# The first two pairs of a fused linear attention and MLP kernel, cut into single tiles of 128 tokens

## The chip, the cores and the metric

The kernel runs on one core of one Trainium2 chip. The metric is the device time of one execution in microseconds. The time before is 217.22 us, the median of three runs (215.41, 217.22 and 218.05).

## The reference

Linear attention with a decay per head is followed by a normalised MLP with a residual. `q`, `k`, `v` are float32 of shape (4, 8, 768, 64): batch, heads, tokens, head width.

```python
for b in range(nb):                      # blocks of 64 tokens
    intra = einsum('bhic,bhjc->bhij', qb, kb) * Dmask      # lam ** (i - j), causal
    intra = einsum('bhij,bhjd->bhid', intra, vb)
    inter = einsum('bhid,bhde->bhie', qb * lam_pow, kv_state)
    out[:, :, sl] = intra + inter
    kv_state = lam_block * kv_state + einsum('bhsd,bhse->bhde', kb * rev_pow, vb)
x = attn_out as (4, 768, 512)
xn = (x - mean) / sqrt(var + 1e-6) * g_ln
out = x + max(xn @ w_ch1, 0) @ w_ch2     # 512 -> 2048 -> 512
```

## The kernel before, in words

The 3072 tokens are worked as 12 pairs `u` of 256 tokens (pair `u` is chunk `u // 4` of batch `u % 4`). A pair holds two chunks `ab` of 128 tokens; partition `64 * ab + p` holds two neighbouring tokens `j` of all eight heads. Heads are counted as four pairs `p` of heads, `e` being the odd or even one. The work of one pair goes in steps:

- `load_window` issues k, q and v on SP's queue (pair 0 in two parts of four heads, the others whole), in runs of 512 bytes.
- `in_k`, `in_q`, `in_v` cast to bf16 and scale by powers of the decay (`lam_q`, `lam_v`). q carries the growing power and v the falling one, so a mask of zeros and ones (`keep`) is all that the scores need.
- `transpose_pe` turns k and q over on TensorE, or for later pairs `transpose_dma` through SP's queue.
- `scores`, `mask`, `av` are the part inside a chunk; `kv`, `new_state`, `state_sum`, `inter` are the state of 64 by 64 per head and its use. The sums stand in two PSUM tiles, `po0` for chunk 0 and `po1` for chunk 1. Between the two halves of `inter` a small read (`reader`, L417) makes TensorE wait, unless other work stands there.
- `norm` takes mean and variance (L430, L431) and writes the centred, weighted `xc` (L435); `to_xT` transposes it, on TensorE with a copy by ScalarE (L455, L456) for the first two pairs, by DMA (L451) for the others. `rstd_of` takes the root on ScalarE (L461) and the reciprocal on VectorE (L463); it is wanted only by `finish` (L543), since a positive factor passes through the maximum.
- The MLP of pair `g`: `m1` makes two of the 16 feature blocks for 256 tokens (8 matmuls of 256 columns, L484), `m1.tile(c, i)` four blocks, those of quarter `c` of W1, for the 128 tokens `i` alone (16 matmuls of 128 columns, L496). ScalarE's maximum with zero brings the result to `hT` (L487, L499). `m2` (L522) sums four products per part against one quarter of W2.

W1 and W2 are each loaded in four quarters by `load_w1` and `load_w2` on GpSimd's queue, with a cast to bf16. `behind` puts a small copy on GpSimd in front of such a load, so that the load is issued only when the named tile has landed.

The scheduler is told to keep the order of the code, so each engine gets its instructions in the order in which the code issues them. The first two pairs, with the first MLP products between their steps, are written out by hand; from then on a list `plan` of MLP steps runs, and `after` hangs the attention steps of later pairs behind its places (`add(12, ...)`). Buffers set further waits: four PSUM tiles `mm` serve transposes, states and MLP products alike.

## Time and profile before

| | us |
|---|---|
| median of three runs (lowest, highest) | 217.22 (215.41, 218.05) |
| span of the profiled execution, first to last instruction | 214.9 |
| TensorE busy in the span | 201.9 (94%) |
| VectorE, ScalarE, GpSimd busy | 102.9, 87.1, 79.4 |
| first transposes on TensorE | 6.09 |
| first MLP product (L496) | 15.82 |
| first step of the plan (L484) | 31.09 |
| first product with W2 (L522) | 37.68 |
| last matmul ends | 211.06 |

The span and the times of lines are from one profiled execution; the runs' times are of whole executions without the profiler, so the two differ by what lies around the span and by the spread of the runs: 2.3 us from the span to the median. TensorE is busy nearly all the time from 6 us on, so the times above tell at what point of its work it stands.

### The profile page before, as it was taken

What the parts mean: (1) busy time and instruction counts of PE and PEld (TensorE: products, weight loads), DVE (VectorE), ACT (ScalarE), POOL (GpSimd) and SP (SyncE); (2) the same over time, 40 slices, a digit from 0 to 9 for tenths busy, and PEclk for the clock granted to TensorE, in tenths of its full rate; (3) what the DMA queues carried; (4) which work ended last, traced back from release to release, by engine and by line L of the source; (5) the groups of instructions that cost most, each with busy time, mean ns of one, the idle gap of its engine ahead of it and who ended that gap; (6) DMA issues with size and microseconds to landing.
All of it is one profiled execution on the core that took longest, in us unless ns stands there. A gap on an engine that the chain in (4) does not pass through costs nothing.

```text
span 214.9 us, 6642 instructions
## 1 busy us (share of the span) xinstructions
PE 201.9 (94%) x2884; PEld 138.2 (64%) x2899; DVE 102.9 (48%) x225; ACT 87.1 (41%) x165; POOL 79.4 (37%) x111
## 2 busy tenths in 40 slices
...
GB/s 130 289 272 207 219 263 160 236 284 234 215 303 208 169 229 153 110 215 209 126 220 199 137 230 200 177 203 198 206 246 131 128 27 27 99 52 0 98 3 95
DMA packets 94142, 37.13 MB, mean 173 GB/s; under 512 B 68385, under 2 KB 91169, under 8 KB 94114
## 3 DMA queue, kind: packets, MB, share of 16 engines
...
q0 software_dynamic: 4224, 4.19, 12.4%
q8 instruction: 22, 0.36, 0.7%
q10 hardware_dynamic: 306, 0.14, 0.3%
...
## 4 chain that ended last, share of the span: by engine, by line
PE 75%; DMA 13%; POOL 4%; SPq 3%; DVE 2%; issue 1%; POOLq 0%
PE pm L484 35%; PE pm L522 30%; DMA vin<-in_v_dram 6%; DMA qin<-in_q_dram 4%; SPq L71 3%; DMA kqT<-kq 2%; POOL kq L210 2%; POOL vb L216 2%; PE pm2h L513 2%; PE po L406 1%; PE po L393 1%; PE sc L247 1%; PE po L380 1%; PE sc L327 1%; PE pm1t L496 1%
## 5 line engine op out<-in xcount | busy, mean ns | idle before, releaser
L487 ACT ACTIVATE hT<-pm 128x512 bf16<-128x512 f32 x92 | 54.9, 601 | 91.2 <-PE pm L484 91.0
L484 PE MATMUL pm<-xT,w 128*128 128x256 bf16 x736 | 86.3, 273 | 1.9 <-DMA xT<-xc 1.2
L522 PE MATMUL pm<-w,hT 128*128 128x512 bf16 x353 | 81.1, 379 | 1.0 <-issue 0.3
L484 PEld LDWEIGHTS <-w 128*128 128x128 bf16 x736 | 69.8, 98 | 13.8 <-DMA xT<-xc 1.7
L522 PEld LDWEIGHTS <-hT 128*128 128x128 bf16 x368 | 35.5, 98 | 40.0
L543 DVE SCALAR_TENSOR_TENSOR o<-pm,rstd,x 128x512 f32<-128x512 f32 x23 | 17.1, 748 | 43.5 <-PE pm L522 43.4
L287 POOL TENSOR_TENSOR Sn<-Stmp,lam_s 128x256 bf16<-128x256 f32 x16 | 9.7, 611 | 69.7 <-DVE Stmp L365 49.0
L435 DVE SCALAR_TENSOR_TENSOR xc<-po,mv,g_row 128x512 bf16<-128x512 f32 (+1 forms) x24 | 16.8, 706 | 1.8
L257 DVE TENSOR_TENSOR mA<-sc,keep 128x512 bf16<-128x512 f32 x20 | 13.1, 685 | 6.8 <-PE sc L247 6.7
L428 ACT COPY x<-po 128x512 f32<-128x512 f32 x18 | 9.9, 588 | 11.3 <-PE po L393 5.3
L430 DVE BATCH_NORM_STATS2 stats<-x 128x6 f32<-128x512 f32 x18 | 12.4, 688 | 3.9 <-ACT x L428 3.9
L417 DVE COPY seen<-po 128x8 f32<-128x8 f32 x18 | 2.3, 162 | 23.2 <-PE po L406 23.2
L216 POOL TENSOR_TENSOR vb<-vin,lam_v 128x1024 bf16<-128x1024 f32 (+1 forms) x7 | 11.8, 1696 | 3.7 <-DMA vin<-in_v_dram 3.7
L210 POOL TENSOR_TENSOR kq<-qin,lam_q 128x512 bf16<-128x512 f32 x10 | 10.3, 1045 | 7.0 <-DMA qin<-in_q_dram 7.0
L210 POOL TENSOR_TENSOR kq<-qin,lam_p 128x512 bf16<-128x512 f32 x12 | 12.3, 1042 | 0.9 <-DMA qin<-in_q_dram 0.7
L216 POOL TENSOR_TENSOR vb<-vin,lam_p 128x1024 bf16<-128x1024 f32 x6 | 11.4, 1896 | 1.7 <-DMA vin<-in_v_dram 1.7
L199 POOL CAST kq<-kin 128x512 bf16<-128x512 f32 (+1 forms) x18 | 10.3, 599 | 0.6 <-DMA kin<-in_k_dram 0.6
L333 DVE TENSOR_TENSOR mA<-sc,keep 128x512 bf16<-128x512 f32 x12 | 8.2, 681 | 1.4 <-PE sc L327 1.4
L406 PE MATMUL po<-Sn,kqT 64*64 64x64 bf16 x216 | 7.4, 199 | 0.0
L224 PE MATMUL tp<-ident,kq 128*128 128x128 bf16 x48 | 6.2, 277 | 0.3 <-ACT kq L199 0.2
L406 PEld LDWEIGHTS <-kqT 64*64 64x64 bf16 x304 | 5.3, 108 | 1.5 <-issue 1.5
L224 PEld LDWEIGHTS <-kq 128*128 128x128 bf16 x48 | 4.1, 120 | 3.2 <-DVE kq L199 1.5
...
## 6 DMA issues: line engine op xcount, KB each, us to landing
...
```

What stands on the lines that cost most here:

```text
L199: (eng.copy if eng is nc.scalar else eng.tensor_copy)(dst[:, :, :, j], src[:, :, :, j])
L210: eng.tensor_tensor(dst[:, :, :, j], src[:, :, :, j], lq[:, :, :, j:j + 1].to_broadcast([128, n, 2, D]), op=ALU.mult)
L216: eng.tensor_tensor(st[u]["vb"][:, hs], qkv_in[u]["v"][:, hs], lv.to_broadcast([128, n, 2, D]), op=ALU.mult)
L224: nc.tensor.transpose(tp[:, i, j, :], s["kq"][:, a, p, j], ident)
L257: nc.vector.tensor_tensor(s[f"mA{hf}"][:, e], s[f"sc{hf}"][e], kp[:, None, :, :].to_broadcast([128, 2, 2, 128]), op=ALU.mult)
L406: nc.tensor.matmul(s["po"][ab][half[jq], 2 * p + e, :], lhsT=qT[half[e], p, jq, half[ab]], rhs=s["S"][ab][jq][half[e], p, :], start=False, ...
L430: nc.vector.bn_stats(stats, po if early else x)
L435: nc.vector.scalar_tensor_tensor(xc[:, sl], in0=po[:, sl], scalar=mv[:, 0:1], in1=g_row[:, sl], op0=ALU.subtract, op1=ALU.mult)
L484: nc.tensor.matmul(pm[:, b, :], lhsT=w1[n // W2K][:, kk, (n % W2K) * 128:(n % W2K + 1) * 128], rhs=xT_of[g][:, kk, 0:N], start=(b == 0 and ...
L487: nc.scalar.activation(hT[:, u * NB:(u + 1) * NB, 0:N], pm, ACT.Relu)
L522: nc.tensor.matmul(acc[i], lhsT=hT[:, kk, i * 128:(i + 1) * 128], rhs=w2[kk // W2K][:, kk % W2K, :], start=(kk == 0), stop=(kk == KB - 1))
L543: nc.vector.scalar_tensor_tensor(o[:, ab], in0=a, scalar=rstd[:, ab:ab + 1], in1=x[:, ab], op0=ALU.mult, op1=ALU.add)
```

## The change

Pairs 0 and 1 are no longer worked as pairs but as four tiles of 128 tokens. In such a tile the lower half of the partitions holds heads 0 to 3 and the upper half heads 4 to 7 of the same 64 token pairs. `load_tiles` loads k, q and v of a tile by one DMA per half: 24 on SP's queue for the two pairs, where there were six for pair 0 and three for pair 1. New helpers do each step for one tile: `tile_k`, `tile_q` and `tile_v` on 512 elements of each partition; `tile_T` four transposes; `tile_scores`, `tile_av`, `tile_kv` half the matmuls of a pair each. The two PSUM tiles `po0` and `po1` now each hold four heads of both tiles of a pair. `tile_norm` takes its statistics and `xc` in two parts of 256, and `tile_keep_x` copies x to SBUF on ScalarE in two parts. `tile_xT` has one PSUM tile per half, copied by ScalarE and by VectorE.

The mask of one set of heads is done by VectorE from PSUM as before (`mask(u, ab, (0,))`), of the other by a copy on ScalarE and a product in bf16 on VectorE (`tile_mask_act`).

The order written by hand is new. The MLP products of pair 0 and the first of pair 1 are all made by `m1.tile`, with the loop over the 128-row blocks of W1 outside. The constants for pairs from 2 on (`lam_q`, `lam_v`, `lam_p`), the first square root and both `rstd_of` move to the end of the hand-written part, ahead of `in_k` of pair 2. The first quarter of W1 is loaded in two DMAs, quarter 1 follows `tile_v(0, 0)` on GpSimd's queue, quarters 2 and 3 stand around `tile_v(1, 0)`; all of W2 is loaded after quarter 3 of W1 has landed and after both second states. The load of pair 4 moves from the hand-written part to behind place 13 of the plan, and the attention steps of pair 2 move one place back. ScalarE's table for logarithm and exponential is loaded first of all.

The core of the diff follows. Not shown are `open_tiles`, `by_head`, `tile_kv` and `tile_norm`, which are told above, a constant, and the removed lines of the hand-written order.

```diff
+    def load_tiles(u):
+        got = {name: inp.tile([128, H, 2 * D], F32, tag=name + "in", name=name + "in") for name in "kqv"}
+        cc, b = divmod(u, B)
+        qkv_in[u] = {}
+        for name, f in got.items():
+            qkv_in[u][name] = f.rearrange("p (c h) (j d) -> p c h j d", c=2, j=2)
+        src = dict(k=k, q=q, v=v)
+        for ab in range(2):
+            lo = cc * W + ab * C
+            for name in "kqv":
+                dst = got[name].rearrange("p (c h) x -> p c h x", c=2)
+                for hg in range(2):
+                    nc.sync.dma_start(dst[half[hg], ab],
+                                      src[name][b, hg * 4:hg * 4 + 4, lo:lo + C, :].rearrange("h (p j) d -> p h (j d)", j=2))
...
+    def load_w1_rows(c, i):
+        src = moe_w_ch1[i * 256:(i + 1) * 256, c * W1C:(c + 1) * W1C]
+        nc.gpsimd.dma_start(w1[c][:, 2 * i:2 * i + 2], src.rearrange("(k p) f -> p k f", p=128))
...
+    nc.scalar.preload_act_table_set("natural_log_exp_and_others")
     lam_b = const.tile([128, H], F32)
     nc.scalar.dma_start(lam_b, lam[None, :].to_broadcast([128, H]))
-    load_window(0, parts=2)
+    load_tiles(0)
...
+    lnlam_t = const.tile([128, 4], F32)
+    for hg in range(2):
+        nc.scalar.activation(lnlam_t[half[hg]], lam_b[half[hg], hg * 4:hg * 4 + 4], ACT.Ln)
+    lam_tq = const.tile([128, 4, 2], F32)
+    nc.scalar.activation(lam_tq[:, :, 0], lnlam_t, ACT.Exp, scale=e_q)
+    nc.scalar.activation(lam_tq[:, :, 1], lnlam_t, ACT.Exp, scale=e_q1)
+    lam_tv = const.tile([128, 4, 2], F32)
     lnlam = const.tile([128, H], F32)
-    nc.scalar.activation(lnlam, lam_b, ACT.Ln)
     lam_q = const.tile([128, H, 2], F32)
-    nc.scalar.activation(lam_q[:, :, 0], lnlam, ACT.Exp, scale=e_q)
...
+    def tile_k(u, ab, eng):
+        src = qkv_in[u]["k"][:, ab]
+        dst = by_head(st[u]["kq"][:, ab, 0])
+        (eng.copy if eng is nc.scalar else eng.tensor_copy)(dst, src)
+    def tile_q(u, ab, eng):
+        eng.tensor_tensor(by_head(st[u]["kq"][:, ab, 1]), qkv_in[u]["q"][:, ab],
+                          lam_tq[:, :, :, None].to_broadcast([128, 4, 2, D]), op=ALU.mult)
+    def tile_v(u, ab, eng):
+        src = qkv_in[u]["v"][:, ab].rearrange("p h j d -> p (h j) d")
+        lv = lam_tv.rearrange("p h j -> p (h j)")[:, :, None]
+        eng.tensor_tensor(st[u]["vb"][:, ab].rearrange("p h j d -> p (h j) d"), src, lv.to_broadcast([128, 8, D]), op=ALU.mult)
+    def tile_T(u, ab, i, copy):
+        s = st[u]
+        tp = mm_tile([128, 2, 2, 128], BF16, "tp")
+        for a in range(2):
+            for j in range(2):
+                nc.tensor.transpose(tp[:, a, j, :], s["kq"][:, ab, i, j, a], ident)
+        copy(s["kqT"][:, ab, i], tp)
+    def tile_scores(u, ab):
+        s = st[u]
+        kT, qT = s["kqT"][:, ab, 0], s["kqT"][:, ab, 1]
+        sc = [ps.tile([128, 2, 2, 128], F32, tag="sc", bufs=2, name=f"sc{e}") for e in range(2)]
+        s[f"mA{ab}"] = wk.tile([128, 2, 2, 2, 128], BF16, tag=f"mA{ab}", name=f"mA{ab}")
+        for a in range(2):
+            for jk in range(2):
+                for hg in range(2):
+                    for e in range(2):
+                        nc.tensor.matmul(sc[e][half[hg], a, jk, :], lhsT=kT[half[e], a, jk, half[hg]],
+                                         rhs=qT[half[e], a, :, half[hg]],
+                                         start=(a == 0 and jk == 0), stop=(a == 1 and jk == 1), skip_group_check=True)
+        s[f"sc{ab}"] = sc
+    def tile_mask_act(u, ab, e):
+        s = st[u]
+        m = s[f"mA{ab}"][:, e]
+        nc.scalar.copy(m, s[f"sc{ab}"][e])
+        kp = keep_h.rearrange("p a b t -> p a (b t)")
+        nc.vector.tensor_tensor(m, m, kp[:, None, :, :].to_broadcast([128, 2, 2, 128]), op=ALU.mult)
+    def tile_av(u, ab, heads=(0, 1)):
+        s = st[u]
+        if "po" not in s:
+            s["po"] = [ps.tile([128, 2, 4, D], F32, tag=f"po{hg}", name=f"po{hg}") for hg in range(2)]
+        for e in heads:
+            for a in range(2):
+                for j in range(2):
+                    for jq in range(2):
+                        for hg in range(2):
+                            nc.tensor.matmul(s["po"][hg][half[jq], ab, 2 * a + e, :],
+                                             lhsT=s[f"mA{ab}"][half[hg], e, a, j, half[jq]],
+                                             rhs=s["vb"][half[hg], ab, 2 * a + e, j],
+                                             start=(e == 0 and a == 0 and j == 0), stop=False, skip_group_check=True)
...
+    def tile_state_first(u):
+        s = st[u]
+        Sn = wk.tile([128, NP, D], BF16, tag="S", bufs=12, name="Sn")
+        for p in range(NP):
+            nc.scalar.activation(Sn[:, p], s["pk0"][p // 2][:, p % 2], ACT.Identity, scale=lam_s[:, p:p + 1])
+        s["S"] = [(None, None), (Sn, Sn)]
+        state[u % B] = Sn
+    def tile_state_sum(u):
+        s = st[u]
+        tmp = wk.tile([128, NP, D], F32, tag="Stmp", name="Stmp")
+        for hg in range(2):
+            pr = slice(2 * hg, 2 * hg + 2)
+            nc.vector.tensor_tensor(tmp[:, pr], s["pk1"][hg], state[u % B][:, pr], op=ALU.add)
+        s["tmp"] = tmp
+    def tile_state_second(u):
+        Sn = wk.tile([128, NP, D], BF16, tag="S", bufs=12, name="Sn")
+        decay(nc.gpsimd, Sn, st[u].pop("tmp"))
+        state[u % B] = Sn
+    def tile_inter(u, first):
+        s = st[u]
+        qT = s["kqT"][:, 1, 1]
+        S = s["S"][1][0]
+        for a in range(2):
+            for jq in range(2):
+                for hg in range(2):
+                    e = first if hg == 0 else 1 - first
+                    nc.tensor.matmul(s["po"][hg][half[jq], 1, 2 * a + e, :], lhsT=qT[half[e], a, jq, half[hg]],
+                                     rhs=S[half[e], 2 * hg + a, :],
+                                     start=False, stop=(first == 1 and a == 1), skip_group_check=True)
+        if first == 0:
+            for hg in range(2):
+                seen = wk.tile([128, 4], F32, tag="seen", name="seen")
+                nc.vector.tensor_copy(seen, s["po"][hg][:, 1, :, 0])
...
+    def tile_keep_x(u, ab, copy):
+        s = st[u]
+        for hg in range(2):
+            copy(s["x"][:, ab, hg * 256:hg * 256 + 256], s["po"][hg][:, ab].rearrange("p h d -> p (h d)"))
+    def tile_xT(u, ab):
+        s = st[u]
+        g = u
+        if ab == 0:
+            xT_of[g] = gp.tile([128, KA, GT * 128], BF16, tag="xT", bufs=3, name="xT")
+        dst = xT_of[g][:, :, ab * 128:(ab + 1) * 128]
+        for h, copy in enumerate((nc.scalar.copy, nc.vector.tensor_copy)):
+            xt = mm_tile([128, 2, 128], BF16, "xt")
+            for kk in range(2):
+                nc.tensor.transpose(xt[:, kk, :], s["xc"][:, ab, (2 * h + kk) * 128:(2 * h + kk + 1) * 128], ident)
+            copy(dst[:, 2 * h:2 * h + 2], xt)
...
-            for b in range(W2K):
-                for kk in range(KA):
+            for kk in range(KA):
+                for b in range(W2K):
...
+    load_tiles(1)
+    open_tiles(0)
+    tile_k(0, 0, nc.vector)
+    tile_T(0, 0, 0, nc.scalar.copy)
     keep_busy(1, "po0")
     for j in range(2):
+        nc.scalar.activation(lam_tv[:, :, j], lnlam_t, ACT.Exp, scale=e_v[:, j:j + 1])
+    tile_q(0, 0, nc.vector)
+    tile_T(0, 0, 1, nc.vector.tensor_copy)
+    nc.scalar.copy(g_row, g_all)
+    behind(qkv_in[0]["k"][:, 0, 0, 0, 0:1])
+    for i in range(2):
+        load_w1_rows(0, i)
+    tile_v(0, 0, nc.gpsimd)
+    load_w1(1)
+    tile_q(0, 1, nc.gpsimd)
+    tile_v(0, 1, nc.gpsimd)
+    tile_k(0, 1, nc.scalar)
+    tile_scores(0, 0)
+    mask(0, 0, (0,))
+    tile_mask_act(0, 0, 1)
+    tile_T(0, 1, 0, nc.scalar.copy)
+    tile_av(0, 0, (0,))
+    tile_av(0, 0, (1,))
+    tile_T(0, 1, 1, nc.scalar.copy)
+    tile_kv(0, 0)
+    nc.scalar.activation(lnlam, lam_b, ACT.Ln)
     ln_p = lnlam.rearrange("p (a two) -> p a two", two=2)
     for e in range(2):
         nc.scalar.activation(lam_s[half[e]], ln_p[half[e], :, e], ACT.Exp, scale=float(C))
+    tile_state_first(0)
+    tile_norm(0, 0)
+    tile_scores(0, 1)
+    tile_xT(0, 0)
+    mask(0, 1, (0,))
+    tile_mask_act(0, 1, 1)
+    tile_keep_x(0, 0, nc.scalar.copy)
+    m1a, m2a = mlp(0)
+    m1b, m2b = mlp(1)
+    tile_av(0, 1)
+    tile_inter(0, 0)
+    tile_inter(0, 1)
+    m1a.tile(0, 0)
+    tile_norm(0, 1)
+    open_tiles(1)
+    tile_k(1, 0, nc.scalar)
+    behind(qkv_in[1]["k"][:, 0, 0, 0, 0:1])
+    load_w1(2)
+    tile_v(1, 0, nc.gpsimd)
+    load_w1(3)
+    tile_xT(0, 1)
+    tile_T(1, 0, 0, nc.vector.tensor_copy)
+    m1a.tile(1, 0)
+    tile_q(1, 0, nc.vector)
+    tile_keep_x(0, 1, nc.scalar.copy)
+    m1a.tile(0, 1)
+    tile_T(1, 0, 1, nc.vector.tensor_copy)
+    m1a.tile(1, 1)
+    tile_scores(1, 0)
+    tile_k(1, 1, nc.scalar)
+    tile_q(1, 1, nc.gpsimd)
+    tile_v(1, 1, nc.gpsimd)
+    mask(1, 0, (0,))
+    tile_mask_act(1, 0, 1)
+    tile_T(1, 1, 0, nc.scalar.copy)
+    tile_av(1, 0)
+    tile_kv(1, 0)
+    tile_norm(1, 0)
+    tile_T(1, 1, 1, nc.scalar.copy)
+    tile_state_first(1)
+    tile_scores(1, 1)
+    tile_keep_x(1, 0, nc.scalar.copy)
+    tile_kv(0, 1)
+    tile_xT(1, 0)
+    mask(1, 1, (0,))
+    tile_mask_act(1, 1, 1)
+    m1a.tile(2, 0)
+    tile_state_sum(0)
+    m1a.tile(2, 1)
+    tile_av(1, 1)
+    tile_inter(1, 0)
+    tile_inter(1, 1)
+    tile_norm(1, 1)
+    behind(w1[2][:, 0, 0:1])
+    load_window(2, after_pool=True)
+    tile_state_second(0)
+    m1b.tile(0, 0)
+    m1b.tile(1, 0)
+    tile_keep_x(1, 1, nc.scalar.copy)
+    tile_kv(1, 1)
+    tile_state_sum(1)
+    tile_state_second(1)
+    m1b.tile(2, 0)
+    tile_xT(1, 1)
+    m1a.tile(3, 0)
+    nc.scalar.activation(lam_q[:, :, 0], lnlam, ACT.Exp, scale=e_q)
     nc.vector.tensor_tensor(lam_q[:, :, 1], lam_q[:, :, 0], lam_b, op=ALU.mult)
+    for j in range(2):
+        nc.scalar.activation(lam_v[:, :, j], lnlam, ACT.Exp, scale=e_v[:, j:j + 1])
     nc.vector.tensor_copy(e_p[:, 0:1], io_p)
     nc.vector.tensor_scalar(e_p[:, 1:2], e_p[:, 0:1], -1.0, None, op0=ALU.mult)
     for i in range(2):
         nc.scalar.activation(lam_p[:, i], lnlam, ACT.Exp, scale=e_p[:, i:i + 1])
     sqrt_first = const.tile([128, 1], F32)
+    nc.scalar.activation(sqrt_first, eps_t, ACT.Sqrt)
+    rstd_of(0)
+    rstd_of(1)
+    behind(w1[3][:, 0, 0:1])
     load_w2(0)
     open_window(2)
     in_k(2, nc.vector)
     load_w2(1)
+    in_q(2, nc.gpsimd)
     load_w2(2)
+    in_v(2, nc.gpsimd)
     load_w2(3)
     load_window(3, after_pool=True)
...
-    plan = [(m1b, n) for n in range(m1b.count // NWC, m1b.count)]
+    plan = [(m1a.tile, 3, 1), (m1b.tile, 3, 0)] + [(m1b.tile, c, 1) for c in range(NWC)]
...
-    add(0, (transpose_pe, 2, 0, (0, 1, 2, 3)))
-    add(2, (transpose_pe, 2, 1, (0, 1, 2, 3)))
-    add(2, (new_state, 0, 1, nc.gpsimd), (new_state, 1, 1, nc.gpsimd))
-    add(4, (s1b, 2))
-    add(6, (s2, 2))
-    add(8, (s0, 2))
-    add(10, (s3, 2))
-    add(12, (s4, 2), (p4, 2), (p0, 3, nc.vector), (transpose_dma, 3))
+    add(1, (transpose_pe, 2, 0, (0, 1, 2, 3)))
+    add(3, (transpose_pe, 2, 1, (0, 1, 2, 3)))
+    add(5, (s1b, 2))
+    add(7, (s2, 2))
+    add(9, (s0, 2))
+    add(11, (s3, 2))
+    add(13, (s4, 2), (p4, 2), (load_window, 4), (p0, 3, nc.vector), (transpose_dma, 3))
```

## The prediction

> **What bounds the kernel now.** I read the stages first, cut where TensorE (PE) passes a landmark. Columns: stretch, length, busy time of PE, PEld, DVE, ACT, POOL, then granted clock, DMA share, GB/s.
>
> ```profile
> 6.09:15.82 9.73, 8.55 (x174) 5.94 (x174) 7.08 (x20) 6.72 (x20) 5.10 (x9) 1.00 1.19 276
> 15.82:31.09 15.27, 14.26 (x276) 12.38 (x276) 10.54 (x23) 9.96 (x20) 7.24 (x10) 1.00 1.17 237
> ...
> 53.81:55.02 1.21, 0.01 (x2) 0.03 (x2) 0.75 (x1) 0.00 (x0) 1.21 (x2) 1.00 1.20 233
> 55.02:211.06 156.04, 154.69 (x2165) 106.18 (x2176) 72.02 (x152) 59.24 (x107) 49.31 (x65) 1.00 0.78 155
> ```
>
> From 55 us on PE works 154.69 of 156.04 us, and the change adds nothing there. It can gain only in the start and in one hole of 1.2 us. What moves the plan's start (31.09) moves the end as much, unless a hole takes it up.
>
> Second, PE's timeline, which gives the pace of the start:
>
> ```profile
> 15.82 1.86 PE L496 MATMUL pm1t<-xT,w 128*128 128x128 bf16 x16 [0.32 <-ACT xT L456]
> ...
> 18.85 1.05 PE L496 MATMUL pm1t<-xT,w 128*128 128x128 bf16 x16
> ...
> 31.09 1.04 PE L484 MATMUL pm<-xT,w 128*128 128x256 bf16 x8
> ...
> 55.02 3.65 PE L484 MATMUL pm<-xT,w 128*128 128x256 bf16 x32 [1.20 <-DMA xT<-xc]
> ```
>
> The same 16 matmuls take 1.86 us at 15.82 and 1.05 at 18.85, though the clock column says 1.00 for both: until some 18.5 us PE runs at half pace. Sixteen matmuls of 128 columns issue in 0.89 us at full pace, eight of 256 (L484) in 0.87. So cutting MLP products into tiles costs PE nothing.
>
> Third, the chain of waits before 31 us:
>
> ```profile
> 7.58 12.64 DMA vin<-in_v_dram
> ...
> 20.29 1.91 POOL vb L216
> ...
> 22.24 0.45 PE pk L281 x32
> ```
>
> It runs over the landing of pair 1's v. That is the one place where data hold the old start; elsewhere PE waits for VectorE and ScalarE. The new order must be costed on those two.
>
> **The first tile.** Tile (0,0) needs 256 KB each of k, q and v, where the first part before needed as much (k used at 5.04), so I take the same landing. The two loads of tables (1.28 each) become one, issued early: logarithm and powers follow lam's landing at 4.28 by 2×0.21 + 2×0.25, ready at 5.2 instead of 6.3. PE's transposes wait for the product L164 until 6.1 as before. Then q by VectorE (0.69, taken from the mask of the same size; bounds 0.42 and 0.84 from half the size), a copy 0.42, first scores at 8.0 (before 9.05). Masks 0.69 on VectorE, 0.56 + 0.46 over ScalarE; `av` from 9.4 to 10.7. GpSimd has `behind` 0.2, two issues of W1 (0.47 each), `tile_v` 1.04, the issue of W1's quarter 1 (0.8) and `tile_q(0,1)` 1.04, so q of the second tile is ready at 10.7, its copy at 12.0, its scores at 12.0. `norm` costs 1.85 on VectorE and xT(0,0) is transposed at 12.4, against 14.41 (L455). So far the change wins **2 us**.
>
> **Where that is lost.** PE has `av(0,1)` and both halves of `inter` ahead of the first product. ScalarE, after the copy of q, owes 3 constants (0.6), four parts of the state (0.94, L306), xT's half (0.36, between 0.33 and 0.58) and the mask's copy 0.56: 14.5. VectorE's part of the mask 0.46 ends at 15. `av` 0.9, `inter` 0.2, two reads L417 with nothing between (0.6 of PE standing; before, `inter(0)` of pair 0 had transposes there), `inter`: the first L496 at 16.1 to 17.0, I take **16.5**, 0.7 later than before.
>
> There is one thing more in the way. po0 and po1 now hold both tiles, so `av(0,1)` may have to wait for ScalarE's two copies of x of tile (0,0) (0.68) in the same PSUM tile; nothing before shows whether. Between 0 and 0.7 us; the 16.5 contains half. The Trainium skill, PSUM — Partial Sum Buffer, section PSUM bank collisions raise a hardware error, says that accesses of two engines to one bank and quadrant must be kept apart by semaphores, even at other columns. By that rule it is the whole 0.7; no row here shows it.
>
> From 16.5 to the plan PE has 13.1 us of work: ten products (1.66 + 9×0.89 = 9.7), 16 transposes of q and k (0.9), 12 of xc (0.7), scores 0.4, `av` 0.65, `kv` 0.4, `inter` 0.3. And it stands, as ScalarE's order is now L499, then the next tile's k: 1.0 before T of k(1,0), 1.2 before T of k(1,1); 0.6 for the second mask of (1,0); 0.85 for the copy of q(1,1) (T, ScalarE 0.58, scores at once); 0.5 between the halves of xT(1,0); 0.9 before `m1a.tile(2,0)`, whose buffer is still with ScalarE behind the states and x; 0.55 at the second pair of L417. Sum 5.6; in the old order the same stretch stands some 2.7. Plan at 16.5 + 13.1 + 5.6 = **35.2**: **+4.1 us** (34.5 to 36).
>
> **The constants put last.** `in_k(2)` on VectorE, and with it the transposes of pair 2 behind place 1 of the plan, now stands after `rstd_of(1)`. That waits for ScalarE:
>
> ```profile
> 20.55 1.28 ACT L659 ACT_TABLE_LOAD   x1
> 21.84 0.20 ACT L659 ACTIVATE sqrt_first<-eps_t 128x1 f32<-128x1 f32 x1
> ```
>
> From the end of `m1a.tile(3,0)`: maximum 0.6, five powers 1.3, table 1.28, root 0.2, two roots 0.6, reciprocal 0.17, two casts of k 0.85, hand-overs 0.2: 5.2. PE has two products (1.8) to cover it, so it stands for 3.2 to 3.4: **+3.2 us**. Before, the table load lay at 20.55 under full buffers. Whoever removed this stall would meet W2: its first load now comes after `state_second(1)`, about at the plan's start, instead of at 18.36; W1's and W2's loads took 7.4 to 11.0 to land, and part 0 of `m2` is wanted 6.5 after the plan's start. Beside the 3.2 that costs 0 to 1.3, I take 0; without them 0.9 to 4.5.
>
> **What costs nothing, and its cover.** SP issues 24 loads at 0.46 to 0.51 each, until 13.4 instead of 9.2; k(1,0) is not used before 18 us. W1's quarter 1, issued at 8.9 and landing by 8.2 to 11.0 later, is wanted at 19.5: cover 0 to 2. Quarters 2 and 3 (issued 12 and 17.5) are wanted at 28 and 34. Pair 2's load still follows quarter 2 at about 23; its k, landing near 30, is used after 38. The new constants are smaller than those that they replace.
>
> **The hole at 53.81.** VectorE's last xc of pair 2 is done at 48.36, but SP is still issuing pair 4, and the transposes queue behind its data:
>
> ```profile
> 47.05 1.93 SPq L71 DMA_DIRECT2D vin<-in_v_dram  x1
> 49.08 3.64 SPq L451 DMA_TRANSPOSE xT<-xc  x2
> ```
>
> With pair 4 loaded after them, the hole (1.2) and the wait at 59.27 for kqT (0.23) can go; one place later (0.87) eats into less than what SP gains. Between 0 and 1.4, I take **-1.4**. Pair 4 is wanted from place 38 on, some 14 us after its landing.
>
> **Sum.** 4.1 + 3.2 - 1.4 = +5.9 us on the profiled span of 214.9, so 220.8. The median of the runs stands 2.3 above that span (0.5 to 3.1); I carry 2.3: **223.1**, rounded to 223.0. Own range 220.8 to 225.0: plan ±0.8, bank ±0.35, hole 0 to 1.4, quarter 1 of W1.
>
> **Rivals.**
> - *PE's clock falls again* (0.24): the stand of 3.2 us slows PE as the end of the run does, where the last matmul ends at 211.06:
>
> ```profile
> 210.02:213.43 3.41, 1.00 (x10) 0.65 (x7) 0.48 (x1) 0.00 (x0) 0.00 (x0) 1.00 0.49 118
> 213.43:214.90 1.47, 0.00 (x0) 0.00 (x0) 0.00 (x0) 0.00 (x0) 0.00 (x0) 0.50 0.00 0
> ```
>
>   The clock is at 0.50 2.4 us after the last work. The first stretch from 15.82 needed 3 us of products to come up, which costs half of that, 1.6: **224.6**; a later rise in the start adds 0.77 per product. Against it: the stand lies between dense work. The Trainium skill (TensorE: Matmul & The Clock Gate, Why this matters for your kernels) allows gaps up to about 3 us; by it this stand is on the edge.
> - *The scalar chain is hidden* (0.12): PE comes late enough to the transposes that VectorE is there first. Then -3.2, but W2 takes at least 0.9 of it: **220.7**.
> - *Not slower* (0.14): the gain of 2 us is kept. If `av(0,1)` does not wait for ScalarE, the first L496 comes at 13.4, as soon as W1's first rows have landed, and PE then stands 2.7 as before: plan at 13.4 + 13.1 + 2.7 = 29.2, so 214.9 - 1.9 + 3.2 - 1.4 + 2.3 = **217.1**. It decides from a first L496 before 13.6 on. For it: the transposes at 12.4. Against: 1.6 us of ScalarE's constants and states stand between. Faster by over 2% it is only if the scalar chain hides too: 217.1 - 3.2 = 213.9 is still 1.5%.
>
> **How the numbers follow.** The forecast, slower at 223.0, has 0.50. Runs of this kernel tell a difference of about 2%, 4.3 us, from none; that line lies at 221.6. Of the forecast's 0.50, 0.37 lies above it; with the clock's 0.24 that is 0.61 slower. Of *not slower*, 0.03 goes to more than 2% faster, as the chain's pieces may err together; the rest is 0.36. The range goes from 217.4, which leaves out most of *not slower*, to 226.0, which holds the clock's case and a late rise.
>
> **What would show it.** Right: the first L496 after 16, the plan's first products after 34, ScalarE's table load next to them with PE standing about 3 us before L224 of pair 2, no hole before the 32 products L484 of pair 2. Wrong: a first L496 near 13, PE without stands over 0.5 us from there on, or roots done before PE is through its two products.

## The result and the profile after

The changed kernel takes 235.94 us (median of four runs, 234.35 to 237.3) against 216.39 before (four runs). The ratio is 1.0905, 95% interval 1.0819 to 1.099: slower by some 19.5 us, where 223.0 was forecast. The profiled execution has a span of 235.1 us and a time of 236.85. The ratios below leave out runs that were some per cent slower than the others of their kernel, and as the profiled run of kernels 7 and 14 was such a one, no plan start is given for these two.

The stages, cut at the same landmarks (stretch, length, busy time of PE, PEld, DVE, ACT, POOL, granted clock, DMA share, GB/s):

```profile
5.79:20.19 14.40, 7.05 (x151) 4.72 (x150) 5.66 (x14) 6.46 (x19) 6.28 (x9) 1.00 1.05 227
20.19:41.15 20.96, 17.70 (x354) 15.79 (x349) 11.13 (x31) 11.78 (x28) 5.70 (x10) 1.00 0.65 143
...
43.10:47.31 4.21, 0.01 (x1) 0.00 (x1) 2.62 (x4) 2.67 (x6) 4.19 (x5) 0.75 1.18 189
47.31:54.57 7.26, 7.21 (x97) 6.84 (x97) 0.28 (x1) 3.88 (x6) 0.70 (x2) 0.68 1.19 198
...
74.58:78.13 3.55, 0.00 (x0) 0.10 (x1) 0.42 (x1) 0.26 (x1) 2.48 (x2) 1.00 1.19 185
...
85.00:231.00 146.00, 145.66 (x1980) 98.72 (x1976) 68.84 (x146) 54.45 (x99) 43.15 (x59) 1.00 0.70 146
```

From 85 us on PE is full, as it was before from 55 on. All the loss lies ahead: PE is busy for only half of the stretch up to its first MLP product, and it stands twice, for 4.21 and 3.55 us. PE's timeline gives the landmarks:

```profile
20.19 1.89 PE L680 MATMUL pm1t<-xT,w 128*128 128x128 bf16 x16
...
40.26 2.84 PE L680 MATMUL pm1t<-xT,w 128*128 128x128 bf16 x48
47.31 1.26 PE L253 MATMUL tp<-ident,kq 128*128 128x128 bf16 x8 [4.21 <-DVE kq L228]
...
54.57 1.90 PE L706 MATMUL pm<-w,hT 128*128 128x512 bf16 x8
...
70.55 3.66 PE L668 MATMUL pm<-xT,w 128*128 128x256 bf16 x32
78.13 0.42 PE L276 MATMUL sc<-kqT 64*64 64x128 bf16 x16 [3.55 <-DMA kqT<-kq]
```

The plan starts with the second 16 of the 48 products at 40.26, at 41.15. Against before:

| | before | after | added |
|---|---|---|---|
| plan start | 31.09 | 41.15 | 10.1 |
| plan start to first product with W2 | 6.59 | 13.42 | 6.8 |
| from there to the first-layer products of pair 2 | 17.34 | 15.98 | -1.4 |
| from there to the scores of pair 3 | 4.25 | 7.58 | 3.3 |
| from there to the last matmul | 151.79 | 153.07 | 1.3 |

The rows add to 20.1 us. The 6.8 is the stand of 4.21 and a stretch of half clock, the 1.3 another such stretch, as the clock column says between two of its steps:

```profile
45.17:52.00 6.83, 4.64 (x43) 4.46 (x44) 2.42 (x2) 2.22 (x4) 2.84 (x3) 0.50 1.18 187
...
79.30:82.72 3.42, 3.42 (x32) 2.16 (x30) 1.68 (x4) 1.19 (x2) 3.03 (x5) 0.50 1.10 361
```

In the chain of waits, the data of pair 1's v no longer hold the start; the second tile's q of pair 0 do, which SP began to issue at 6.24 and which GpSimd used at 13.59:

```profile
6.90 6.54 DMA qin<-in_q_dram
...
13.59 1.04 POOL kq L513
```

The same tile's k comes late as well. In ScalarE's order its cast stands ahead of the copy for the first tile's mask, so that the first `av` waits too (12.21, forecast at 9.4):

```profile
11.01 0.62 ACT L510 CAST kq<-kin 128x512 bf16<-128x512 f32 x1 [3.14 <-DMA kin<-in_k_dram]
```

SP's queue shows the issues, of 256 KB before (the first and the last load of the two pairs, the last of 512 KB), of 128 KB after (two to a row):

```profile
0.81 0.46 SPq L71 DMA_DIRECT2D kin<-in_k_dram  x1
...
7.58 1.65 SPq L71 DMA_DIRECT2D vin<-in_v_dram  x1
```

```profile
4.92 1.27 SPq L109 DMA_DIRECT2D kin<-in_k_dram  x2
...
18.80 1.69 SPq L109 DMA_DIRECT2D vin<-in_v_dram  x2
```

All engines at the first stand:

```profile
42.95 1.28 ACT L876 ACT_TABLE_LOAD   x1
...
44.66 0.35 DVE L492 RECIPROCAL rstd<-std 128x2 f32<-128x2 f32 x2 [2.07 <-ACT std L490]
...
44.93 2.66 DVE L228 CAST kq<-kin 128x512 bf16<-128x512 f32 x2
45.05 1.91 POOL L245 TENSOR_TENSOR vb<-vin,lam_v 128x1024 bf16<-128x1024 f32 x1
```

The table, the roots and the reciprocals stand in front of the casts as forecast. But the two casts, priced at 0.85 together, take 2.66 (the first alone 2.32), beside a product on GpSimd.

SP's queue ahead of the second stand:

```profile
68.65 1.38 SPq L71 DMA_DIRECT2D vin<-in_v_dram  x1
70.14 4.50 SPq L260 DMA_TRANSPOSE kqT<-kq  x2
```

The window that was moved away from the transposes of xT(2) now lies ahead of those of kq(3).

### The profile page after: what moved, and what is told of

Same layout as the page of the kernel before. It is cut to its first block, busy times and chain, and to the rows that moved or that the text cites. A ratio compares the mean times of both kernels' runs of the same rounds, so it can differ in the third digit from the quotient of the medians.

```text
span 235.1 us, 6907 instructions
## 1 busy us (share of the span) xinstructions
PE 208.5 (89%) x2995; PEld 144.3 (61%) x2995; DVE 104.5 (44%) x234; ACT 89.7 (38%) x180; POOL 79.4 (34%) x111
## 4 chain that ended last, share of the span: by engine, by line
PE 83%; DMA 5%; ACT 4%; SPq 3%; DVE 2%; issue 1%; POOL 0%; POOLq 0%; DVEq 0%
PE pm L706 34%; PE pm L668 30%; PE pm1t L680 7%; DMA qin<-in_q_dram 3%; SPq L109 2%; DMA kqT<-kq 2%; PE pm2h L697 1%; PE sc L276 1%; PE po L435 1%; PE po L422 1%; DVE kq L228 1%; PE po L409 1%; PE tp L526 1%; PE sc L356 1%; ACT Sn L583 1%
## 5 line engine op out<-in xcount | busy, mean ns | idle before, releaser
L671 ACT ACTIVATE hT<-pm 128x512 bf16<-128x512 f32 x80 | 47.9, 599 | 89.8 <-PE pm L668 89.8
L668 PE MATMUL pm<-xT,w 128*128 128x256 bf16 x640 | 75.4, 276 | 0.0
L668 PEld LDWEIGHTS <-w 128*128 128x128 bf16 x640 | 61.9, 99 | 10.5 <-DVE Smid L391 0.2
L680 PE MATMUL pm1t<-xT,w 128*128 128x128 bf16 x256 | 20.2, 251 | 0.5 <-ACT xT L649 0.5
L286 DVE TENSOR_TENSOR mA<-sc,keep 128x512 bf16<-128x512 f32 x20 | 13.3, 685 | 15.6 <-PE sc L276 13.7
L680 PEld LDWEIGHTS <-w 128*128 128x128 bf16 x256 | 18.9, 116 | 0.7 <-issue 0.6
L464 DVE SCALAR_TENSOR_TENSOR xc<-po,mv,g_row 128x512 bf16<-128x512 f32 x18 | 13.5, 751 | 1.6
L459 DVE BATCH_NORM_STATS2 stats<-x 128x6 f32<-128x512 f32 x18 | 12.4, 687 | 4.1 <-ACT x L457 4.1
L683 ACT ACTIVATE hT<-pm1t 128x512 bf16<-128x512 f32 x16 | 9.4, 595 | 12.2 <-PE pm1t L680 12.1
L228 POOL CAST kq<-kin 128x512 bf16<-128x512 f32 x16 | 9.4, 613 | 7.1 <-PE pm L668 7.1
L526 PE MATMUL tp<-ident,kq 128*128 128x128 bf16 x32 | 4.5, 286 | 6.2 <-ACT kq L510 4.6
L239 POOL TENSOR_TENSOR kq<-qin,lam_q 128x512 bf16<-128x512 f32 x8 | 8.2, 1043 | 0.4 <-DMA qin<-in_q_dram 0.2
L526 PEld LDWEIGHTS <-kq 128*128 128x128 bf16 x32 | 2.6, 125 | 9.1 <-ACT kq L510 5.2
```

Of the source, the lines that this page charges most:

```text
L228: (eng.copy if eng is nc.scalar else eng.tensor_copy)(dst[:, :, :, j], src[:, :, :, j])
L239: eng.tensor_tensor(dst[:, :, :, j], src[:, :, :, j], lq[:, :, :, j:j + 1].to_broadcast([128, n, 2, D]), op=ALU.mult)
L286: nc.vector.tensor_tensor(s[f"mA{hf}"][:, e], s[f"sc{hf}"][e], kp[:, None, :, :].to_broadcast([128, 2, 2, 128]), op=ALU.mult)
L459: nc.vector.bn_stats(stats, po if early else x)
L464: nc.vector.scalar_tensor_tensor(xc[:, sl], in0=po[:, sl], scalar=mv[:, 0:1], in1=g_row[:, sl], op0=ALU.subtract, op1=ALU.mult)
L668: nc.tensor.matmul(pm[:, b, :], lhsT=w1[n // W2K][:, kk, (n % W2K) * 128:(n % W2K + 1) * 128], rhs=xT_of[g][:, kk, 0:N], start=(b == 0 and ...
```

## The experiments

Eighteen kernels ran in five batches, each beside the kernel before on the same chip. "Ratio" is to that, with its 95% interval; plan start is from one profile each. Before itself is at 31.09, the changed kernel at 41.15.

| | edit | us | ratio | plan start |
|---|---|---|---|---|
| 1 | 9 of 24 loads on ScalarE's queue | 244.13 | 1.1281 (1.1207 to 1.1355) | 49.1 |
| 2 | 12 dummy matmuls | 236.97 | 1.0971 (1.0877 to 1.1066) | 41.7 |
| 3 | cast of k(2) first | 232.99 | 1.0748 (1.0661 to 1.0836) | 40.4 |
| 4 | window 4 behind kq(3) | 238.74 | 1.104 (1.0952 to 1.1127) | 44.0 |
| 5 | W1 behind pair 0 | 237.55 | 1.097 (1.0866 to 1.1074) | 42.9 |
| 6 | window 4 early | 233.87 | 1.0832 (1.0707 to 1.0956) | 42.0 |
| 7 | 3 + 5 + 6 | 232.73 | 1.075 (1.0649 to 1.0851) | |
| 8 | before, window 4 moved | 220.9 | 1.0201 (1.0102 to 1.03) | 32.2 |
| 9 | 12 loads of 256 KB | 234.83 | 1.0797 (1.0719 to 1.0875) | 39.9 |
| 10 | 9 + 3 + 6 | 229.62 | 1.0563 (1.0486 to 1.0641) | 40.0 |
| 11 | before, v(4) later | 217.16 | 1.0041 (1.0007 to 1.0075) | 30.7 |
| 12 | v(2) later on GpSimd | 237.08 | 1.0917 (1.084 to 1.0995) | 41.6 |
| 13 | 3, W2 and windows 3, 4 early | 226.72 | 1.0492 (1.0435 to 1.0549) | 42.6 |
| 14 | v(2) on VectorE | 235.24 | 1.086 (1.0808 to 1.0912) | |
| 15 | 30 dummy matmuls | 235.75 | 1.0899 (1.0856 to 1.0942) | 39.9 |
| 16 | before, 8 dummy matmuls | 216.71 | 1.0009 (0.9976 to 1.0042) | 33.4 |
| 17 | 13 + 9, one quarter of W1 | 222.14 | 1.0308 (1.024 to 1.0376) | 38.8 |
| 18 | before, 24 loads | 219.87 | 1.0196 (1.013 to 1.0262) | 36.1 |

One caution for the last column. Up to the plan, the changed kernel and runs 3, 4, 6 and 12 have the same code, and they start it at 40.4 to 44.0, by when the loads happen to land. A difference of 2 us there in one profile proves nothing. In runs 9, 10 and 17 the rows of the first two pairs land in other places than the arithmetic expects, and run 17 loads a quarter of W1 alone, so of these only the time counts.

### 1 to 4: each suspect alone

**1.** `load_tiles` puts its transfers for the upper half of the partitions in a list, and ScalarE issues them, those of pair 0 behind its first powers, those of pair 1 behind `g_row`.

```diff
-                    nc.sync.dma_start(dst[half[hg], ab],
...
+                    if hg == 1 and (u, ab) != (0, 0):
+                        later.append((dst[half[hg], ab], part))
+                    else:
+                        nc.sync.dma_start(dst[half[hg], ab], part)
...
+        for dst, src in later:
+            nc.scalar.dma_start(dst, src)
```

> The changed kernel with 9 of SyncE's 24 loads of the first two pairs (second half of the partitions; of the first pair's second tile and of the whole second pair) issued by ScalarE in its idle stretches at 4.4 and 7.9 us; same transfers, same sizes. Theory (24 issues of 0.63 us one after another on SyncE make the tiles late): SyncE is done at about 10.5 us instead of 20.5, k(0,1) is used at 8 to 9 instead of 11.0, v of the second pair's second tile at 15 to 19 instead of 26.0, the plan starts 4 to 7 us earlier than 41.15, time about 231 (229 to 233). Rival (the order of work on ScalarE and VectorE sets the start, as the prediction had it): the loads land earlier and the plan starts within 1 us of 41.15, time 235 to 237.

Neither: 8 us worse. SyncE was done at 15.5, but ScalarE stood in its own queue for an earlier load to land. The waits of the run (who, on whom; total, times, longest):

```profile
ACT kqT L538 <- DMA kin<-in_k_dram: 8.2, 1, 8.2
```

Here the issues on an engine that also computes stopped its computing. So this run tells nothing of the 24 issues.

**2.**

```diff
     tile_scores(0, 0)
+    keep_busy(7, "po0")
...
+    keep_busy(3, "sc")
     tile_T(0, 1, 1, nc.scalar.copy)
     tile_kv(0, 0)
+    keep_busy(2, "sc")
```

> The changed kernel with 12 matmuls of 512 columns, whose result nobody reads, in TensorE's waits of the first pair: seven behind the first scores, three ahead of the transposes of q(0,1), two behind the first key-value products. Theory (the start also pays for a TensorE clock that stays at half until 28.1): the clock is full before 18 us, the first-layer products from 20 on step at half the time, the plan starts 1.5 to 3.5 us earlier, time 232 to 234. Rival (TensorE only waits in the start, its own clock hides in the waits): plan start within 0.7 us of 41.15, or later by the dummies, time 235 to 237.

The rival. The clock came up at 11.3, fell again at 14.7 in the waits, and stayed at half until 28.4.

**3.**

```diff
+    open_window(2)
+    in_k(2, nc.vector)
     nc.scalar.activation(lam_q[:, :, 0], lnlam, ACT.Exp, scale=e_q)
...
-    nc.scalar.activation(sqrt_first, eps_t, ACT.Sqrt)
-    rstd_of(0)
-    rstd_of(1)
...
-    open_window(2)
-    in_k(2, nc.vector)
...
+    add(6, (rstd_of, 0), (rstd_of, 1))
```

> The changed kernel with the cast of k(2) on VectorE ahead of the constants, and the square-root table, stds and reciprocals of the first two pairs behind plan place 6. Theory (the stand of 4.21 us at 43.10 is the constants-last chain, and it costs a stretch of half clock as well): stand gone or under 0.7, no record of half clock at 45 to 52, first second-layer product 6 to 7 us earlier than 54.57, time 228 to 231. Rival (the stand is only traded for one at the next place, transposes of q(2)): a stand of 2 us or more at plan place 3, time 233 to 236.

The stand was gone, nothing took its place at the plan's third step, and the first product with W2 came at 47.06 instead of 54.57. But the time fell by 3 us, not by 7: the stand at the scores of pair 3 was still there, at 67.1, now of 4.0 us.

**4.**

```diff
-    add(13, (s4, 2), (p4, 2), (load_window, 4), (p0, 3, nc.vector), (transpose_dma, 3))
+    add(13, (s4, 2), (p4, 2), (p0, 3, nc.vector), (transpose_dma, 3), (load_window, 4))
```

> The changed kernel with the load of window 4 behind the DMA transposes of kq(3) in SyncE's queue instead of ahead of them; nothing else. Theory (the stand of 3.55 us at 74.58 comes from the 1.5 MB of window 4 that were put ahead of those transposes when the load was moved behind plan place 13): transposes issued at about 67.5 instead of 70.1 and landed at about 74, stand under 0.8, no half clock at 79 to 83, time 230 to 232. Rival (window 3 is late because the second layer's weights were issued late on GpSimd, so kq(3) is late): stand stays 3 us or more, time 234 to 237.

PE no longer stood for kqT(3); it stood for xT(3), at 90.2:

```profile
PE pm L668 <- DMA xT<-xc: 3.6, 1, 3.6
```

The stand was handed on. In this profile the start, too, came 2.9 us later than in the changed kernel, with the same code up to there; whether the edit itself costs time is not shown.

### 5 to 8: W1, window 4, and the sum

**5.**

```diff
-    behind(qkv_in[0]["k"][:, 0, 0, 0, 0:1])
-    for i in range(2):
-        load_w1_rows(0, i)
     tile_v(0, 0, nc.gpsimd)
-    load_w1(1)
     tile_q(0, 1, nc.gpsimd)
     tile_v(0, 1, nc.gpsimd)
+    for i in range(2):
+        load_w1_rows(0, i)
+    load_w1(1)
```

> The changed kernel with the first two quarters of W1 issued on GpSimd behind the first pair's q and v of the second tile, instead of between them. Theory (the first pair's second tile waits because a quarter of W1 shares the 16 DMA engines with it from 6 us on): k(0,1) is used before 9.7 us instead of 11.0, GpSimd waits under 1.5 us for q(0,1) instead of 4.3, first first-layer product at 17 to 19 instead of 20.2, plan start 2 to 4 us earlier than 41.15, time 231 to 234. Rival (24 issues of 0.63 us on SyncE are what is late, whoever else moves data): k(0,1) within 0.5 us of 11.0, and since W1 now comes later the first first-layer product is at 21 or later, time 236 to 239.

Half right: k(0,1) was transposed at 9.59 instead of 11.68, and GpSimd waited 1.3 us for q(0,1). But PE, ready for the first product at 17.0, then waited 2.0 us for W1, and 3.7 in all for the first four products, and pair 1's last v was used at 28.5 instead of 26.0. What one load gains, the next loses. And with W1 out of the way the loads alone came in at 186 GB/s from 2 to 10 us, hardly faster than the 163 of the changed kernel.

**6.**

```diff
     load_window(3, after_pool=True)
+    load_window(4)
...
-    add(13, (s4, 2), (p4, 2), (load_window, 4), (p0, 3, nc.vector), (transpose_dma, 3))
+    add(13, (s4, 2), (p4, 2), (p0, 3, nc.vector), (transpose_dma, 3))
```

> The changed kernel with window 4 loaded right behind window 3, as before the change, instead of behind plan place 13. Theory (from 66 us on the DMA transposes of kq(3), xT(3) and kq(4) and the 1.5 MB of window 4 want the same stretch; moving only their order, as the fourth run did, hands the stand on from 75 to 90): window 4 has landed by 65, no stand over 0.6 us at the scores of pair 3 nor at the products of pair 3, no half clock after 55, time 230 to 232. Rival (another stretch pays, the transposes of xT(2) behind the longer queue at 64): a stand of 1.5 to 3 us before the first-layer products of pair 2, time 233 to 236.

No stand at pairs 2 and 3; the profiled span fell by 3.9 us, the median by 2, which is not clear of the noise (the intervals of the two ratios overlap).

**7.** The edits of 3, 5 and 6 together.

> The changed kernel with three edits together: W1 behind the first pair's data, the cast of k(2) ahead of the constants with the stds behind plan place 6, window 4 right behind window 3. Theory (three independent causes, each of its own size): 3 + 5 + 5 us less than 235.9, time 221 to 225. Rival (they share one cause, and what one gives the next takes back): time 227 or more.

The rival: no better than 3 alone. A stand of 4.3 us came up before the first-layer products of pair 2.

**8.** Of the whole change, only the move of window 4, in the kernel before.

```diff
-    load_window(4)
...
-    add(12, (s4, 2), (p4, 2), (p0, 3, nc.vector), (transpose_dma, 3))
+    add(12, (s4, 2), (p4, 2), (load_window, 4), (p0, 3, nc.vector), (transpose_dma, 3))
```

> The kernel before with one edit of the change: window 4 loaded behind the transposes of xT(2), ahead of the DMA transposes of kq(3). Theory (the move itself opens the stand at the scores of pair 3): the stand of 1.2 us before the first-layer products of pair 2 goes, the one at the scores of pair 3 grows from 0.2 to 3 to 4 us, with or without a stretch of half clock behind it, time 218 to 221 against 216.6. Rival (the move is the gain of 1.4 us that the prediction counted, and the new stand came from the changed kernel's late start): time 214.8 to 215.6.

As the theory had it: the hole of 1.2 us went, a stand of 2.7 us at the scores of pair 3 came, and 3.4 us of half clock behind it. The move that the prediction booked as a gain of 1.4 costs this kernel 2% (1.0 to 3.0).

```profile
61.43 0.42 PE L247 MATMUL sc<-kqT 64*64 64x128 bf16 x16 [2.68 <-DMA kqT<-kq]
```

### 9 to 12: the size of the loads, and GpSimd beside VectorE

**9.**

```diff
-                dst = got[name].rearrange("p (c h) x -> p c h x", c=2)
-                for hg in range(2):
-                    nc.sync.dma_start(dst[half[hg], ab],
-                                      src[name][b, hg * 4:hg * 4 + 4, lo:lo + C, :].rearrange("h (p j) d -> p h (j d)", j=2))
+                hs = slice(ab * 4, ab * 4 + 4)
+                nc.sync.dma_start(got[name][:, hs], source(src[name], u, hs))
```

> The changed kernel with each tile's k, q and v of the first two pairs fetched by one transfer of 256 KB over all 128 partitions instead of two of 128 KB over 64 each: 12 issues on SyncE instead of 24, same bytes, same buffers, same order. The rows that land are those of the old layout, so the first two pairs are computed on misplaced tokens and only the time is read. Theory (24 issues of 0.63 us hold the loads to some 0.2 MB per us until 16 us, and everything behind them is late): SyncE is done before 10 us, 1.5 MB of q, k and v have landed by 10 us instead of 1.0, the first first-layer product is at 16 to 18 instead of 20.2, the plan starts at 35 to 37.5 instead of 41.15, time 229 to 232. Rival (the sum of bytes, W1 among them, or the order of work on ScalarE and VectorE, holds the start): SyncE done early, but plan start 39.5 to 42, time 234 to 237.

The rate of the loads did what was expected, though SyncE was done at 13.3, not before 10. The same stretch of before, of the changed kernel and of this run:

```profile
2.00:10.00 8.00, 5.48 (x35) 2.47 (x36) 3.71 (x16) 6.12 (x14) 4.32 (x10) 1.00 1.01 259
```

```profile
2.00:10.00 8.00, 4.26 (x27) 1.81 (x27) 3.09 (x10) 2.42 (x9) 4.80 (x9) 1.00 0.76 163
```

```profile
2.00:10.00 8.00, 4.29 (x30) 2.16 (x31) 2.61 (x10) 3.12 (x11) 4.13 (x9) 1.00 0.96 251
```

The last column goes from 163 back to 251 GB/s. Yet the plan started only 1.3 us earlier than in the changed kernel's profile, and the time is not clearly lower. One part of the answer is the first tile: its scores came at 9.10 instead of 7.92. In all three runs with whole transfers (9, 10, 17) lam, a load of 4 KB, was used from 5.0 to 5.1 us on; in the changed kernel and every other run with halves it was 3.4 to 3.7. So the halves had made the first tile early and the later ones late. Another part stands in the timeline of VectorE and GpSimd:

```profile
10.44 2.55 DVE L547 TENSOR_TENSOR mA<-mA,keep_h 128x512 bf16<-128x512 bf16 x1
...
10.64 1.05 POOL L511 TENSOR_TENSOR kq<-qin,lam_tq 128x512 bf16<-128x512 f32 x1
11.65 1.04 POOL L517 TENSOR_TENSOR vb<-vin,lam_tv 128x512 bf16<-128x512 f32 x1
```

A mask product that takes 0.43 us elsewhere took 2.55 and ended 0.3 us after GpSimd's second product. The earlier data let GpSimd start its products just there, and `av` waited for the mask. The Trainium skill, SBUF — State Buffer, section SBUF: two separate sides, says that VectorE (with two inputs in SBUF, or in a mode that uses two ports) and GpSimd take one pair of ports as a lock: whichever starts first holds it for the whole instruction, and the other stands still. The rows agree on the standing still. They do not agree on who wins: VectorE's product starts 0.20 us ahead of GpSimd's by the profile and still ends after two of them. Nor is the length fixed: in run 17 the mask product started at 10.52, ahead of the second of the same two products, and took 0.72, and that product took 1.22.

**10.** The edits of 9, 3 and 6 together.

> The changed kernel with three edits: the 12 transfers of 256 KB of the run before (misplaced tokens in the first two pairs, only the time is read), the cast of k(2) ahead of the constants with the stds behind plan place 6, window 4 right behind window 3. Theory (start, stand at the plan's first place and stand at pair 3 are three causes that add): 4 to 6 for the start, 6.8 for the stand and its half clock, 4 for window 4 off 235.9: 218 to 222. Rival (the late weights of the second layer or the DMA transposes make a new stand, as in the run with three edits before): 224 or more.

The rival: no first stand, but 4.0 us before the first-layer products of pair 2. Run 7 has the same cast and window 4, but half loads (and W1 behind them). Run 10 is better by 1.9% of the time before, 4 us, and the intervals do not overlap.

**11.** In the kernel before, only v of window 4 behind the transposes of kq(3).

```diff
-    load_window(4)
+    load_one(4, "k")
+    load_one(4, "q")
...
-    add(12, (s4, 2), (p4, 2), (p0, 3, nc.vector), (transpose_dma, 3))
+    add(12, (s4, 2), (p4, 2), (p0, 3, nc.vector), (transpose_dma, 3), (load_one, 4, "v"))
```

> The kernel before with one edit: of window 4 only v is loaded behind the DMA transposes of kq(3); k and q stay where they are. It is the gain that the prediction counted for the move of window 4, without the queue in front of kq(3). Theory: the transposes of xT(2) are issued 1.5 to 2 us earlier than 49.08, the stand of 1.2 us before the first-layer products of pair 2 goes, none opens at pair 3, time 214.6 to 215.8 against 216.2. Rival (the stand is only handed on, or v comes late for pair 4): 216 to 218.

The rival again: the hole at 53.8 closed, and one of 1.5 us opened at the products of pair 3 (xT(3), 70.2). Not faster than before.

**12.** `in_v(2, nc.gpsimd)` put behind `load_window(3)`.

> The changed kernel with the product for v(2) on GpSimd behind the issue of W2 and window 3, so that no GpSimd arithmetic runs beside VectorE's cast of k(2). Theory (VectorE's cast took 2.32 us instead of 0.42 because GpSimd's product of 1.91 us held it up): both casts 0.4 to 0.6 us, the stand at 43.1 shrinks from 4.2 to 2.1 to 2.6 us, time 231.5 to 234.5. Rival (the cast was slow for another reason, the landing of window 2 or the constants): cast stays above 1.5 us, stand 4 us, time 235 to 237.

The edit missed: the start came at 41.6, so the product still ran beside the cast (46.27 against 45.40), and the cast took 3.09. It tells only that the two go together, and not quite that: the cast had 0.87 us before the product started, twice what it takes alone. What held it until then, while GpSimd issued W2, stays open.

### 13 to 16: the origin of the stands, and the clock

**13.**

```diff
     load_window(2, after_pool=True)
+    behind(w1[3][:, 0, 0:1])
+    for c in range(4):
+        load_w2(c)
+    load_window(3, after_pool=True)
+    load_window(4)
     tile_state_second(0)
```

with the cast of k(2) first, as in 3, and the loads taken out at their old places.

> The changed kernel with the four loads of W2 and windows 3 and 4 issued right behind window 2, ahead of the second states on GpSimd, and with the cast of k(2) ahead of the constants as in the third run. Theory (W2, window 3 and window 4 crowd the DMA transposes because GpSimd issues them only after the second state at 40 us, while the DMA engines stand idle from 34 to 42): W2 landed by 45, window 4 by 57, no stand over 0.7 us at any DMA transpose, time 223 to 227. Rival (the stand at a DMA transpose comes from the transposes and the stores themselves): a stand of 2.5 us or more at pair 2, 3 or 4 remains, time 229 to 233 as in the third run.

The theory, though W2 landed near 50 instead of 45. PE has no stand from the plan's start on:

```profile
42.64:63.00 20.36, 20.36 (x313) 12.94 (x311) 9.89 (x22) 9.77 (x20) 12.00 (x12) 1.00 0.96 210
63.00:85.00 22.00, 21.76 (x321) 14.21 (x320) 12.47 (x25) 7.14 (x13) 8.67 (x12) 1.00 1.00 210
```

In the changed kernel GpSimd had waited 8.3 and 3.7 us for the sums of the second states before it issued W2, from 40.5 on. In 34 to 42 us its DMA moved 4 GB/s; here it moved 222:

```profile
34.00:42.00 8.00, 7.64 (x180) 7.26 (x180) 4.24 (x14) 4.95 (x12) 2.79 (x5) 1.00 0.02 4
```

```profile
34.00:42.00 8.00, 6.75 (x157) 5.96 (x156) 4.52 (x16) 4.62 (x12) 1.22 (x2) 1.00 1.20 222
```

So the stands at the transposes come from loads that were issued late, behind the second states, and crowd the transposes. That W2, which stands ahead of window 3 in GpSimd's order, is the one to blame is argued only: this run moved W2, window 3 and window 4 together.

**14.**

```diff
-    in_v(2, nc.gpsimd)
...
-    add(3, (transpose_pe, 2, 1, (0, 1, 2, 3)))
+    add(3, (transpose_pe, 2, 1, (0, 1, 2, 3)), (in_v, 2, nc.vector))
```

> The changed kernel with the product for v(2) on VectorE behind plan place 3 instead of on GpSimd beside the cast of k(2). Theory (VectorE's cast waits for GpSimd's product to end): both casts 0.4 to 0.7 us, stand at 43.1 of 2.3 to 2.9 us instead of 4.2, time 232 to 235. Rival (something else holds the cast): first cast above 1.5 us, time 235 to 238.

The theory, in the stand: VectorE's two casts took 0.42 and 0.75, and PE waited 2.7 us for them instead of 4.2.

```profile
48.94 1.09 DVE L228 CAST kq<-kin 128x512 bf16<-128x512 f32 x2
```

The time is not clearly lower, 235.24 where the theory had at most 235: the stand of 2.7 us still cost a step of half clock, and the stand at pair 3 stayed.

**15.** Eight dummy matmuls before the first real one (as in 16), then nine, seven, two and four in the later waits of pair 0.

> The changed kernel with dummy matmuls of 512 columns in all of TensorE's early waits: eight ahead of the first real one (from 1.5 us), nine behind the first scores, seven ahead of the transposes of q(0,1), two behind the key-value products, four ahead of the second tile's products with v. Theory (half clock until 28 us makes the four first-layer tiles of 20 to 28 us cost 3.3 us more): full clock from before 10 us on and still at 20, first-layer matmuls at 56 ns instead of 105, plan start 2.5 to 3.5 us earlier, time 232 to 234. Rival (the waits are the start, and the clock is lost again in them): half clock at 20 to 26 again, time 235 to 238.

The clock was full from 13.8 to 30.9 and the first-layer products went at 56 ns. From the first one to the plan it took 19.1 us instead of 21.0. But the dummies themselves held back the transposes of k(0,1) to 13.3, and the time is the same. The half clock is worth some 2 us there; run 3, whose clock happened to be full from 23.6 on, took 18.7 for the same stretch. It is more like 3 if one adds what a new step of half clock took back in this run, at 30.9 to 34.3, behind no stand longer than 0.9:

```profile
31.55 3.23 PE L683 MATMUL pm1t<-xT,w 128*128 128x128 bf16 x32 [0.36 <-ACT xT L652]
```

In the changed kernel these 32 products, at 34.08, took 1.95.

**16.**

```diff
+    warm = ps.tile([128, DM], F32, tag="po0", name="warm")
+    for _ in range(8):
+        nc.tensor.matmul(warm, lhsT=ident, rhs=ident[:, None, :].to_broadcast([128, 4, 128]), start=True, stop=True)
     nc.tensor.matmul(g_all, lhsT=ones, rhs=g_one, start=True, stop=True)
```

> The kernel before with eight dummy matmuls of 512 columns ahead of the first real one, while the first loads are under way. Theory (its start, too, runs at half clock until 18.9 us, and TensorE is busy for most of 9 to 19): full clock from before 9 us, first scores as before at 9.05, first first-layer product 1 to 2 us earlier than 15.82, time 214 to 215.5. Rival (loads and the order on ScalarE and VectorE set that start): clock full but time within 0.5 us of 216.6.

The rival: the clock was full from 5.4 to 8.8 only, and the time is the same.

### 17 and 18: loads against order

**17.** Run 13 with the loads of run 9, and `w1` as one tile that stands for all four quarters.

> The run with W2 early, and in addition the 12 transfers of 256 KB (misplaced tokens in the first two pairs) and only the first quarter of W1 loaded, which stands in for all four: 3 of 4 MB of W1 are left out, so only the time is read. Theory (with the loads out of the way the start is still late, by the serial hand-overs from tile to tile, the half clock and GpSimd's products in front of VectorE's): first first-layer product at 17.5 to 19, plan start at 37.5 to 40 against 42.7 in the run with W2 early and 31.09 before the change, time 221.5 to 225. Rival (the loads are the start): first first-layer product before 16.5, plan start at 34 to 36.5, time 217 to 220.5.

The theory. With three quarters of W1 out of the way and q, k and v in whole transfers the first product came at 17.56, the plan at 38.8. By the ratios this is 4 us better than 13.

**18.**

```diff
+        if u < 2:
+            for h in half:
+                nc.sync.dma_start(got[h, hs], source(src, u, hs)[h])
+            return
...
-    load_window(1)
+    load_window(1, parts=2)
```

> The kernel before with the first two pairs loaded as the change does it in size and number, 24 transfers of 128 KB over 64 partitions (12 a pair, in the order k, q, k, q, v, v); same data in the same places, nothing else touched. Theory (issues of 0.63 us each hold back the loads, and W1 gets in between): SyncE done near 20 us instead of 9.2, first first-layer product 3 us or more later than 15.82, time 219.5 to 223. Rival (the order of work absorbs the late loads): time 216 to 218.

The theory: SyncE done at 17.6 instead of 9.2, 174 GB/s from 2 to 10 us instead of 259, first product at 20.63 instead of 15.82.

```profile
20.63 1.87 PE L500 MATMUL pm1t<-xT,w 128*128 128x128 bf16 x16 [0.32 <-ACT xT L460]
```

The Trainium skill, DMA: Bandwidth & Descriptors, section Rules for kernel authors, says that two transfers to the two halves of the partitions do not pay and that one over all 128 should be used. This run agrees and gives the price in this kernel: 2% (1.3 to 2.6).

## Why the prediction was wrong, step by step

The direction was right and the mechanism of the first stand too. Of the 20.1 us in the profile 5.9 had been forecast.

**The loads: the step that failed first.** "What costs nothing" priced 24 issues with the row of 256 KB, 0.46 to 0.51, and had SP done at 13.4; and the first tile "took the same landing". That row holds for the first four transfers alone; in run 9 later ones of the same size took 0.65 to 3.31. An issue of half the bytes over half the partitions took 0.61 to 0.62 (medians), SP was done at 20.5, and the loads came at 163 instead of 259 GB/s. Run 18 shows the cost alone: 4.8 us at the first product, in the old order. First scores at 8.0 (7.92) and xT(0,0) at 12.4 (16.5) show where it bites: in the second tile, whose q GpSimd used at 13.59 and not, as costed, at 9.7, and through the second tile's k, which ScalarE awaits until 11.01 ahead of the first tile's mask.

**The order of work: about right.** The forecast had the first product at 16.5 and the plan 18.7 later, at 35.2. In run 5 PE was ready for the first product at 17.0. With most loads out of the way (17) it came at 17.56 and the plan 21.3 later. There the first scores came at 9.19, 1.2 after the forecast, as in the other runs with whole transfers; without that it would be 16.4, an estimate. And of the 21.3, 2 to 3 us are the clock (3 and 15), which leaves 18 to 19 where 18.7 was forecast. So 35.2 was about what the order alone costs, 4 us; the clock adds 2 to 3, the loads the rest of the 10.1, in keeping with the 4 us that lie between 10 and 7 and between 17 and 13. Loads and order do not simply add: in the old order the loads alone cost 5.0 at the plan's start, and halving their number in the new one gave back 1.3 (9), partly since the first tile then came 1.2 later and GpSimd's products fell upon VectorE's mask.

**The shared PSUM tile: within its bounds.** `av(0,1)` did wait for ScalarE's copies of x; PE stood 1.45 us there. But VectorE's half of the mask was ready only at 18.06, 0.5 before PE started at 18.59, and the second mask 0.04 us after, so the copies held back the first half of the products alone, by about 0.4. The forecast had 0 to 0.7 and counted half. No run took the wait away.

**The constants put last: 4.2 for 3.2.** The chain came as forecast, through table, roots, reciprocals and casts; run 3, which takes it away, takes the stand away. The mis-sized term is the casts, 0.85 forecast, 2.66 measured; with GpSimd's product gone (14) they are 1.09. The chain ahead of them, forecast at 4.35, took 3.8 (41.15 to 44.93), which hid part of the miss. What the forecast saw behind the stand, W2, it priced at 0. No product waited for W2; the price of the late loads came later, at the transposes (13).

**The hole.** The gain of 1.4 came, to the digit, but by luck: the forecast had added the hole of 1.2 and the wait of 0.23 for kqT(3), and that wait did not go. It grew to 3.55: the same move opened 3.3 us at the scores of pair 3 and a step of half clock, 1.3. The forecast counted the queue in front of xT(2) and not that in front of kq(3), the next transposes on the same queue. Run 8 shows the move alone as a loss. Run 13 shows that it need not be one: the window can have landed before either.

**The rival *the clock falls again*** was not a rival but part of the case, twice: 2.4 us after the first stand (run 3 takes 4.90 from the transposes of pair 2 to the first product with W2, the changed kernel 7.26) and 1.3 after the second. Its price of 1.6 was for one step. The limit of about 3 us that the prediction quoted from the Trainium skill (TensorE: Matmul & The Clock Gate, Why this matters for your kernels) was not safe here: run 8 shows a step of half clock behind a stand of 2.7 us, and run 15 one behind no stand over 0.9. Nor did a longer stand always cost one: run 5 stands for 3.7 us at 76.8 and keeps the full clock. *The scalar chain is hidden* and *Not slower* fell with the first product at 20.19.

Nothing beat the kernel before: the two attempts at it gave ratios of 1.0041 (11) and 1.0009 (16). Of the changed kernel with all its loads, 13 is the best, 9 us better and still 4.9% slower than before. What remains there is all in the start. Not settled is how the 10.1 us divides within 2 us, as the start itself moves by 3.7 between profiles of the same code.
